# Segment-recurrent attention beside a gated MLP: output projection by column blocks, casts ahead of the transposes, and PSUM assigned by hand

## The chip, the cores and the metric

The kernel runs on one core of a Trainium2 chip. The metric is device time in microseconds: the median of three runs is 979.2 us (976.85 to 980.56). The engines are TensorE (PE; its weight loads are listed as PEld), VectorE (DVE), ScalarE (ACT), GpSimd (POOL) and SyncE (SP), which issues most DMAs.

## The reference

```python
# x (1,2048,512), mem0 (1,8,512); Wq, Wk, Wv (512,32,128); Wo (32,128,512); segments of 32 tokens
for s in range(64):
    h = concat([mem, x[:, 32*s:32*s+32]])                # 40 rows: 8 of memory, 32 of x
    q, k, v = (einsum('btd,dhe->bhte', h, W) for W in (Wq, Wk, Wv))
    scores = where(mask, q @ k.T * 128**-0.5, -1e9)      # memory rows see all, x rows causally
    o = softmax(scores) @ v
    o = einsum('bhte,hed->btd', o, Wo)
    mem = o[:, :8]; outs.append(o[:, 8:])                # the memory of the next segment
a = concat(outs)
b = gelu(layernorm(x) @ w1 + b1) @ w2 + b2               # 512 -> 1376 -> 512
g = sigmoid((x * gate_w).sum(-1)); return g * a + (1 - g) * b
```

All operands are bf16. The 64 segments are a chain: each needs the eight memory rows that the one before has put out.

## The kernel before

**MLP first.** 16 tiles of 128 tokens are taken two at a time. DVE makes the statistics of x (L114 to L117), ACT a Sqrt and a Tanh (`rstd`, L122), `prep` (L145) normalises and transposes, TensorE multiplies with w1 (L178) and w2 (L172), ACT applies Gelu (L179). `c_all` keeps (1-g)*b in SBUF for all tokens (L188). SP loads all weights in the order written; x lies whole in `x_all`.

**Setup.** Loop buffers are cleared by POOL (L214 and on), and the mask `MkA` is built by some 120 small POOL operations (L228 to L247), in four variants for the four segments of a tile.

**The loop** over 64 segments `s` (T is the tile of 128 tokens, si the segment in it) is emitted in an order written by hand, one fixed stream for each engine; `dve_q`, `act_q` and the generators `fill` and `left` hold work that is dropped in at chosen places (`flush`, `run_fill`).

- Of a segment's 40 rows, 32 (8 of memory, 24 of x) go through `qk_unit` and `v_unit`: the 32 columns of h are the stationary operand in each of the four column quadrants of TensorE, and each quadrant streams one 32-wide quarter of the heads' columns. The last 8 rows of the four segments of a tile (32 rows, the last keys) are computed a tile ahead by `left_qk` and `left_v`, as filler.
- `qk_tr` (L271): DVE transposes a bank of Q or K in 32x32 blocks from PSUM as f32 into `Tt`; ACT or POOL then casts `Tt` into QT or KT (L513), POOL into QL or KL for the last keys (L331).
- `mask_mm` puts the mask into the bank S; `scores` adds, for each of 32 heads, a matmul on the first 32 keys (L413) and one on the last keys of the whole tile (L417), of which the mask leaves this segment's 8.
- ACT takes the exponentials for memory queries (L530) and x queries (L531). TensorE sums them with a block of ones (L533, L534; L544, L545), DVE takes reciprocals (L537, L549), Pm (L539, DVE) and Px (L472, POOL) are the probabilities. `av` multiplies with V per head, main keys (L427) and last keys (L431): at once for the memory queries, a segment later for the x queries. The results go to `UTT` (L548, L485).
- Projection, `wo_unit` (L287): 32 matmuls of 512 columns. Quadrant g takes the heads with i % 4 = g, so the four quadrants hold four partial sums of all 512 columns. They are copied to `wsb` (L565 on DVE, L566 on ACT), and L575 adds the quadrants while transposing the eight memory rows; DVE writes them to the next segment's hT (L576). The x rows wait in `wsb` until a tile is complete; `out_units` adds the quadrants (L361, L370), DVE applies gate and c (L375), and one DMA stores 128 rows (L376).
- PSUM: one pool of seven banks, handed out in turn (`bank`), and one bank for S.

After the loop two sums tell whether a number left its range; a second, safe path (`tc.If`) would then compute all again.

## Time and profile before

| | us |
|---|---|
| median of three runs | 979.2 |
| span of the profiled execution | 978.4 |
| MLP on TensorE, from the first transposes to the last w2 matmul | 17.8 to 108.3 |
| from there to the first Q matmul of segment 0 | 108.3 to 138.2 |
| first Q matmul of segment 0 to that of segment 63 | 138.2 to 952.2 |
| from there to the end | 952.2 to 978.4 |

The page gives no other time of the profiled execution than its span; that lies 0.8 below the median. The page of the profile has busy times by engine, then the chain of work that ended last, then groups of instructions by source line. A row of a timeline has the start, the duration of the merged group, engine, line, operation, tiles (out<-in), the count, and in brackets how long the engine had stood idle before it and for whom.

| group | count | mean ns |
|---|---|---|
| L271 DVE transposes of 128x512 f32 | 256 | 715 |
| L485 ACT copies of U for x rows, 128x256 | 256 | 822 |
| L513 ACT casts to QT and KT, 128x512 | 128 | 618 |
| L549 DVE reciprocals, 128x256 | 64 | 1750 |
| L565, L566 copies of the projection, 128x256 | 66 each | 425, 373 |

### The profile page before, as it was taken

The page shows a single profiled execution, that of the slowest core. Times are in us where ns is not written, and L with a number is a line of the kernel's source. Part 1 is how long each engine was busy: PE and PEld are TensorE (multiplying, and loading weights), DVE is VectorE, ACT ScalarE, POOL GpSimd, SP SyncE. Part 2 cuts the span into 40 slices and gives each one's busy share as a digit, 9 for nine tenths or more (in the row PEclk, how much of TensorE's full clock was granted, in tenths as well). Part 3 has the DMA queues.
Part 4 walks back from the last instruction along what each step waited for, and adds up shares of the span by engine and source line. Part 5 has one row for each costly group of instructions (what it writes and reads, how often), then busy time and mean ns, then how long its engine had stood idle before and what let it go on. Part 6 is the DMA issues. An engine that isn't in the chain of part 4 may idle for free.

```text
span 978.4 us, 53663 instructions
## 1 busy us (share of the span) xinstructions
PE 871.1 (89%) x24969; PEld 518.0 (53%) x24977; DVE 514.7 (53%) x999; ACT 525.9 (54%) x1252; POOL 257.0 (26%) x599
## 2 busy tenths in 40 slices
PE   2999649998999999999999999989899999999996
PEld 1666315555555555555555555555555555555553
DVE  4721416554556555655565555555555545555553
ACT  2655324555555555555555555555555555555564
POOL 1000463222222232223222223222222222232320
PEclk9999779999999999999999999999999999999999
DMA  9960000000000000000000000000000000000000
GB/s 285 422 199 1 12 2 4 9 4 3 16 4 14 4 15 3 15 4 15 4 15 3 15 4 3 15 4 15 3 15 4 15 4 15 3 9 4 10 7 12
DMA packets 14996, 29.65 MB, mean 30 GB/s; under 512 B 1032, under 2 KB 12656, under 8 KB 13232
## 3 DMA queue, kind: packets, MB, share of 16 engines
q1 hardware_dynamic: 14592, 25.90, 7.4%
q8 instruction: 197, 3.23, 1.4%
q0 software_dynamic: 176, 0.27, 0.3%
q14 instruction: 31, 0.25, 0.1%
HBM read 24.06 MB, written 2.10 MB: 27 GB/s over the span
## 4 chain that ended last, share of the span: by engine, by line
PE 78%; ACT 11%; DVE 4%; issue 3%; POOL 2%; DMA 1%; SPq 1%; POOLq 0%; ACTq 0%; DVEq 0%
PE b L265 29%; PE b L287 16%; PE b L276 11%; ACT UTT L485 4%; PE b L427 4%; PE bp L172 4%; PE hp L178 3%; PE b L431 3%; ACT E L530 2%; DVE wsb L565 2%; ACT wsb L566 2%; PE S L417 2%; PE S L413 2%; PE b L533 1%; PE b L544 1%
## 5 line engine op out<-in xcount | busy, mean ns | idle before, releaser
L271 DVE STREAM_TRANSPOSE Tt<-b 128x512 f32<-128x512 f32 (+1 forms) x384 | 225.6, 613 | 111.3 <-PE b L265 82.7
L265 PEld LDWEIGHTS <-hT 128*32 128x32 bf16 x5120 | 144.3, 98 | 111.1 <-issue 14.4
L485 ACT CAST UTT<-b 128x256 bf16<-128x256 f32 x256 | 158.3, 822 | 10.8 <-PE b L431 10.5
L287 PE MATMUL b<-Wo_sb,UTT 128*32 128x512 bf16 x2624 | 161.5, 383 | 2.3 <-ACT UTT L485 1.6
L265 PE MATMUL b<-Wq_sb,hT 128*32 128x512 bf16 x2048 | 137.2, 388 | 18.7 <-POOL hT L396 13.5
L265 PE MATMUL b<-Wk_sb,hT 128*32 128x256 bf16 (+1 forms) x3072 | 137.4, 313 | 0.0
L276 PE MATMUL b<-Wv_sb,hT 128*32 128x512 bf16 x2048 | 134.5, 380 | 0.0
L472 POOL TENSOR_TENSOR Px<-E,R 128x256 bf16<-128x256 bf16 x64 | 43.2, 675 | 345.2 <-DVE R L549 345.2
L513 ACT CAST KT<-Tt 128x256 bf16<-128x256 f32 (+1 forms) x192 | 86.8, 476 | 57.4 <-DVE Tt L271 57.4
L549 DVE RECIPROCAL R<-b 128x256 f32<-128x256 f32 x64 | 112.0, 1750 | 4.5 <-PE b L545 4.5
L566 ACT CAST wsb<-b 128x256 bf16<-128x256 f32 x66 | 24.6, 373 | 157.7 <-DVE wsb L565 157.7
L287 PEld LDWEIGHTS <-UTT 128*32 128x32 bf16 x2624 | 73.0, 106 | 62.4 <-ACT UTT L485 3.5
L427 PEld LDWEIGHTS <-V 32*128 32x128 bf16 x4096 | 68.0, 91 | 58.1 <-DVE Pm L539 29.5
L537 DVE RECIPROCAL R<-b 128x64 f32<-128x64 f32 x64 | 35.7, 558 | 96.6 <-PE b L534 96.6
L513 POOL CAST QT<-Tt 128x512 bf16<-128x512 f32 x64 | 39.4, 616 | 172.4 <-DVE Tt L271 172.4
L431 PEld LDWEIGHTS <-VL 32*128 32x128 bf16 x4096 | 69.1, 91 | 13.4 <-issue 13.3
L548 ACT CAST UTT<-b 128x64 bf16<-128x64 f32 x128 | 28.5, 319 | 79.8 <-PE b L431 79.8
L276 PEld LDWEIGHTS <-hT 128*32 128x32 bf16 x2048 | 53.5, 96 | 25.9
L513 ACT CAST QT<-Tt 128x512 bf16<-128x512 f32 x64 | 39.6, 618 | 50.0 <-DVE Tt L271 49.4
L178 PE MATMUL hp<-yT,w_sb 128*128 128x256 bf16 (+1 forms) x352 | 53.0, 278 | 4.8 <-ACT hTm L179 3.1
L548 DVE CAST UTT<-b 128x64 bf16<-128x64 f32 x128 | 28.4, 301 | 54.0 <-PE b L431 54.0
L179 ACT ACTIVATE hTm<-hp,b_sb 128x256 bf16<-128x256 f32 (+1 forms) x88 | 40.6, 470 | 29.9 <-PE hp L178 29.8
(111 smaller groups left out, 1271.4 us busy)
## 6 DMA issues: line engine op xcount, KB each, us to landing
Wq_sb<-in_A_Wq_dram SPq DMA_DIRECT2D x4, 1024.0 KB, 13.0
Wk_sb<-in_A_Wk_dram SPq DMA_DIRECT2D x4, 1024.0 KB, 18.7
Wv_sb<-in_A_Wv_dram SPq DMA_DIRECT2D x4, 1024.0 KB, 20.2
Wo_sb<-in_A_Wo_dram SPq DMA_DIRECT2D x4, 1024.0 KB, 17.2
out_dram<-o SPq DMA_DIRECT2D x16, 128.0 KB, 1.7
xc<-in_A_x_dram SPq DMA_DIRECT2D x15, 128.0 KB, 2.3
x_all<-in_A_x_dram SPq DMA_DIRECT2D x3, 512.0 KB, 9.2
w_sb<-in_B_w_dram SPq DMA_DIRECT2D x1, 1376.0 KB
```

The lines of the kernel that those rows point to most:

```text
L178: nc.tensor.matmul(hp[:rows, :], lhsT=w1_sb[:, kc, fc * P:fc * P + rows], rhs=yT[:, kc, :], start=(kc == 0), stop=(kc == KC - 1))
L265: nc.tensor.matmul(bk[32 * j:32 * j + 32, 0:n], lhsT=G[:, kc, :], rhs=W5[t][:, kc, h0:h1, j, :], start=(kc == 0), stop=(kc == KC - 1), til ...
L271: nc.vector.transpose(out=Tt[:, 0:n], in_=bk[:, 0:n])
L276: nc.tensor.matmul(bk[32 * j:32 * j + 32, :], lhsT=G[:, kc, :], rhs=Wv5[:, kc, 4 * vb:4 * vb + 4, j, :], start=(kc == 0), stop=(kc == KC - ...
L287: nc.tensor.matmul(bk[32 * g:32 * g + 32, :], lhsT=lhs(i, j), rhs=Wo_sb[:, 4 * i + j, :], start=(j == 0 and i < 4), stop=(j == 3 and i >= ...
L427: nc.tensor.matmul(U[j][:, i, :], lhsT=V[q, i, :], rhs=Pt[q, i, c_main:c_main + n], start=(i == 0), stop=False, skip_group_check=True, til ...
L431: nc.tensor.matmul(U[j][:, i, u0:u0 + 8], lhsT=VL[T % 2][q, i, :], rhs=Pt[q, i, c_left:c_left + 8], start=False, stop=True, skip_group_che ...
L485: nc.scalar.copy(out=UTT[:, :, j, M:40, si], in_=U[:])
L513: (nc.gpsimd.tensor_copy if bi == 2 else nc.scalar.copy)(out=dst, in_=Tv)
L548: (nc.scalar.copy if j % 2 else nc.vector.tensor_copy)(out=UTT[:, :, j, 0:M, sp], in_=Um[j][:])
L549: nc.vector.reciprocal(out=R[:, 8 * NG:].rearrange("p (i q) -> p i q", q=32), in_=sr[:])
L566: nc.scalar.copy(out=wsb[:, 256:512], in_=wp[:, 256:512])
```

## The change

- **Projection.** `wo_group` gives each quadrant g the columns k*128 + 32*g + r (k = 0..3, r = 0..31) and all 32 heads: 128 matmuls of 128 columns. The result W[32g + token, 32k + r] is complete, so a DVE transpose of 128x128 f32 and one cast give the next hT; `wsb`, L575, the selectors and `out_units` go. `combine` applies gate and c to each segment's rows from PSUM, and four DMAs store them, in runs of 32 elements. c goes to DRAM (`c_dr`) and is loaded again by segment; gates per row come from `gseg`. The last rows get the same projection (`wo_left`), 4 loads of c and 16 stores a tile.
- **Q and K.** ACT casts a PSUM bank to bf16 with heads in pairs (`qk_cast`), DVE transposes the pairs as 4-byte elements straight into QT, KT, QL or KL. POOL no longer casts. Four banks of 16 heads stand where three of 16 and two of 8 stood.
- **Last keys.** KL and V's last keys are laid out so that the 8 last keys of four heads fill the 32 rows of one quadrant: one matmul stands for four, in `scores` and in `av`. `Mk` masks out the other heads. V's last keys are regrouped by 8 DMAs a tile.
- **PSUM by hand.** Banks U0 to U3 take Q and K, then U; X1 and X2 take V and the filler; Sb the scores; W the projection and the x queries' sums. Sums are made by quadrants.
- **Order.** The x queries' `av` moves ahead of the sums; filler units are 3, 2 and 3 in a segment and the rest behind them, where they were 5, 2, 1 and 1; x queries' reciprocals go to the start of the next segment; U's x rows are copied right after those of memory.
- **MLP and setup.** 1/sqrt by integer shift and three Newton steps on DVE, without ACT's Sqrt; x in tiles with six buffers; `prep` of the next block and its gates at fc == 1; the mask by DVE and during the MLP; two tables UT, cleared where UTT was. The check of range takes a running minimum of the reciprocals instead of sums out of the exponentials.

```diff
+    def qk_cast(bk):
+        Tb = ew.tile([P, 8, 32, 2], BF16, tag="Tb", bufs=3, name="Tb")
+        nc.scalar.copy(out=Tb[:].rearrange("p a e b -> p a b e"), in_=bk.rearrange("p (a b e) -> p a b e", a=8, b=2))
+    def qk_tr(Tb, dst, hf):
+        nc.vector.transpose(out=dst[:, 8 * hf:8 * hf + 8, 0:32, :].rearrange("p a r b -> p a (r b)").bitcast(FP32),
+                            in_=Tb[:].rearrange("p a e b -> p (a e b)").bitcast(FP32))
...
-    def wo_unit(bk, lhs, u):
-        for (j, i) in HORD[4 * u:4 * u + 4]:
-            g = i % 4
-            nc.tensor.matmul(bk[32 * g:32 * g + 32, :], lhsT=lhs(i, j), rhs=Wo_sb[:, 4 * i + j, :],
-                             start=(j == 0 and i < 4), stop=(j == 3 and i >= NG - 4), tile_position=(0, 32 * g))
+    def wo_group(bk, src, n):
+        j, i = HORD[n]
+        for g in range(4):
+            nc.tensor.matmul(bk[32 * g:32 * g + 32, 0:P], lhsT=src(j, i), rhs=Wo5[:, 4 * i + j, g],
+                             start=(n == 0), stop=(n == H - 1), tile_position=(0, 32 * g))
...
+            for si in range(SPT):
+                nc.sync.dma_start(VP[T % 2][:, si, vb, :], VL[si:P:SPT, 4 * vb:4 * vb + 4, :])
...
+        for j in range(4):
+            a0 = 8 * i2 + j // 2
+            nc.tensor.matmul(Sb[32 * j:32 * j + 32, 4 * i2:4 * i2 + 4, :].rearrange("p i (a b) -> p i a b", b=8)[:, :, 0:7:6, :],
+                             lhsT=KL[T % 2][:, si, j // 2, i2].rearrange("p l a b -> p (l a) b")[:, :, j % 2],
+                             rhs=QT[:, a0:a0 + 7:2, :, j % 2].rearrange("p a (x q) -> p a x q", q=8)[:, :, 0:5:4, :],
+                             start=False, stop=True, skip_group_check=True, tile_position=(0, 32 * j))
...
+    def combine(s):
+        nc.vector.scalar_tensor_tensor(out=o[:], in0=W[:, 0:P], scalar=gseg[:, si, T:T + 1], in1=cs.pop(s)[:], op0=ALU.mult, op1=ALU.add)
+        for g in range(4):
+            nc.sync.dma_start(out4[seg * s:seg * s + RIDE, :, g, :], o[32 * g + M:32 * g + 32, :].rearrange("p (k r) -> p k r", k=KC))
...
+            if s >= 1:
+                av(s - 1, Vs.pop(s - 1), Pxs.pop(s - 1), 64, 32, 0, 32, True)
+            sm = U[0][:, 320:384].rearrange("p (i q) -> p i q", q=8)
+            sums(sm, E, 8, 0, 8, True)
+            run(W1)
+            nc.vector.reciprocal(out=R[:, 0:8 * NG], in_=U[0][:, 320:384])
...
+        for n in range(24):
+            wo_group(W, u_main(s), n)
+        if s < nseg:
+            sums(W[:, P:P + 32 * NG].rearrange("p (i q) -> p i q", q=32), E, 16, 48, 32, False)
+        for n in range(24, H):
+            wo_group(W, u_main(s), n)
+        if s + 1 < nseg:
+            Tm = cw.tile([P, KC, 32], FP32, tag="Tm", name="Tm")
+            nc.vector.transpose(out=Tm[:].rearrange("p k q -> p (k q)"), in_=W[:, 0:P])
+            nc.vector.tensor_copy(out=hn[:, :, 0:M], in_=Tm[:, :, 0:M])
+        if s >= 2:
+            combine(s - 2)
+        if s + 1 < nseg:
+            mask_mm()
+        if s < nseg:
+            run(W3)
```

## The prediction

> **What bounds the kernel now.** I read the page's busy times and chain first, then the table of busy time by stage, then the waits of TensorE, then timelines of single segments.

> ```profile
> span 978.4 us, 53663 instructions
> ...
> PE 871.1 (89%) x24969; PEld 518.0 (53%) x24977; DVE 514.7 (53%) x999; ACT 525.9 (54%) x1252; POOL 257.0 (26%) x599
> ...
> PE 78%; ACT 11%; DVE 4%; issue 3%; POOL 2%; DMA 1%; SPq 1%; POOLq 0%; ACTq 0%; DVEq 0%
> ```

> TensorE is busy 89% and carries 78% of the chain, so its instruction stream sets the time, and the other engines count where TensorE waits for them. The stages, by timelines: the MLP to 108, a gap to 138, 64 segments, an end.

> ```profile
> 108.00:138.00 30.00, 8.71 (x111) 3.77 (x109) 9.97 (x17) 2.61 (x4) 22.37 (x126) 0.65 0.04 10
> ...
> 190.00:952.00 762.00, 713.24 (x22354) 421.43 (x22354) 425.05 (x792) 429.35 (x1048) 210.08 (x421) 0.99 0.03 8
> ```

> Columns are the stretch, its length, then busy time of PE, PEld, DVE, ACT, POOL. In the gap TensorE works 8.7 of 30 us while POOL works 22. In the loop ACT and DVE are each busy 56%.

> The first and the last segment start with these Q matmuls, so 63 segments take 952.22 - 138.24 = 814 us, 12.92 each; the rest is 138.2 ahead and 26.2 behind:

> ```profile
> 138.24 1.90 PE L265 MATMUL b<-Wq_sb,hT 128*32 128x512 bf16 x16 [13.49 <-POOL hT L396]
> ...
> 952.22 1.05 PE L265 MATMUL b<-Wq_sb,hT 128*32 128x512 bf16 x16
> ```

> One segment (from 500.92 to 513.55) shows how its 12.63 us are spent:

> ```profile
> 506.94 0.19 PE L534 MATMUL b<-E,BO 128*128 128x64 bf16 x1
> 507.06 1.05 PE L265 MATMUL b<-Wq_sb,GL 128*32 128x512 bf16 x16
> 507.94 0.39 PE L265 MATMUL b<-Wk_sb,GL 128*32 128x512 bf16 x4
> ...
> 508.26 0.18 PE L427 MATMUL b<-Pm,V 32*128 32x8 bf16 x4
> 508.30 0.17 PE L431 MATMUL b<-Pm,VL 32*128 32x8 bf16 x4
> ...
> 512.35 0.24 PE L575 MATMUL b<-Sel,wsb 128*128 128x8 bf16 x4
> 512.45 0.35 PE L404 MATMUL S<-MkA,ident 128*128 128x448 bf16 x1
> 512.99 0.40 PE L265 MATMUL b<-Wq_sb,GL 128*32 128x512 bf16 x4 [0.19 <-ACT UTT L485]
> 513.55 0.81 PE L265 MATMUL b<-Wq_sb,hT 128*32 128x512 bf16 x9 [0.17 <-ACT UTT L485]
> ```

> Durations include each matmul's latency, so I use differences of starts. Four 512-column matmuls in the four quadrants (a group) take 0.865/4 = 0.216 us, four of 256 columns 0.88/8 = 0.110: by the line through both, four of 128 columns take 0.057. Four tiny ones (8 to 40 columns) take 0.025 to 0.035, 0.031 on average, whatever their width. Each change between quadrant, row-tile and whole-array matmuls adds about 0.1 (506.94 to 507.06 for a 64-column matmul). After L404 TensorE has two holes, both ended by the new memory rows: L404's 448 columns are streamed by 512.64, yet Q starts at 513.55 with only 0.22 of filler between.

> **The change on TensorE, per segment.** Kept: Q and K 3.46, V 1.73, mask 0.19. Scores go from 64 to 40 matmuls, 0.50 to 0.31. Each attention-times-V goes from 64 to 40, 0.48 to 0.31, twice. Sums 0.38 to 0.20. The gather L575 (0.10) goes, and so does the output assembly (L361, L370; two groups a tile, 0.11 a segment). The output projection turns 8 groups of 512 columns (1.73) into 32 groups of 128, 32 x 0.057 = 1.82. Filler is 24 groups a tile for the last keys' Q, K and V (5.2), input transposes 0.2 and the last rows' projection 1.82: 7.2 a tile, 1.8 a segment. Sum after: 3.46 + 1.73 + 0.19 + 0.31 + 0.62 + 0.20 + 1.82 + 1.80 = 10.1. The same count before is 10.95, so waits and mode changes are 2.0 of its 12.92.

> **Waits after.** Mode changes fall to four, 0.4. Between row sums and Pm stand the reciprocal (0.56) and the product (0.29): 1.32 from sums to the first row-tile matmul (506.94 to 508.26). After the change 3 filler units (0.65) stand there instead of 5, so about 0.5 of wait. The copies of U take 0.54 from the last matmul to the second copy's start on DVE and 0.43 of filler covers it: 0.1. At the end the chain is shorter: projection, one DVE transpose of 128x128, one cast, Q. The transposes of 256 and 512 columns take 0.41 and 0.72, so 0.25 for 128; with 0.2 for latency ahead, 0.06 between, 0.15 for the cast and 0.17 behind, 0.85. Mask (0.19) and the three filler units left (0.65) fill 0.84 of it, so nothing is left. Without that filler, as in the last tile, 0.65 would show. Sum: 10.1 + 0.4 + 0.5 + 0.1 = 11.1.

> **ACT** gains work: it casts every Q and K bank and writes with a 4-byte step, which no row shows. From below, a contiguous 512-element copy, 0.56 in a row of them. From above, the U copies with an 8-byte step:

> ```profile
> 504.89 0.73 ACT L513 CAST KT<-Tt 128x256 bf16<-128x256 f32 x2 [0.59 <-DVE Tt L271]
> ...
> 512.19 2.47 ACT L485 CAST UTT<-b 128x256 bf16<-128x256 f32 x4
> ```

> Four strided copies take 2.47, one 0.82, so 0.55 apart; contiguous ones 0.33 (0.73 - 0.40). The step costs 0.22/256 = 0.86 ns an element, so 1.00 us for 512. I take 0.78, as the step lies between the two rows. ACT then has per segment U copies 2.6, V 1.0, exp 0.5 (its two accumulator reads go, 0.39), casts 4 x 0.78 = 3.1, last keys 1.05: 8.2 of 11.1. At 0.78 the fourth cast and its transpose end at 4.9 us into the segment, just as TensorE comes to the second half of the scores (scores start after Q, K and 24 V matmuls, 4.75): I add 0.1. At 1.00 the two last-key casts, which stand ahead of the four in half the segments, push it out by 1.5: 0.9 on average, +0.8 over what I take. **DVE** loses 3.5 of transposes from PSUM (225.6 in 64 segments) and gains about 2.1 of them from SBUF (five at 0.41), a minimum and the gating (0.45 and 0.25): under 7 us. **POOL** loses its 0.62 casts. **SP** issues 49 DMAs a tile in place of two: at 0.34 to 0.43 each (out L376, x_all L73) 5 us a segment; who waits is in the third rival. One more 0.1 is for the few slow segments (12.92 is the mean, 12.83 the steady tile). Taken: 11.3 a segment, 63 x 11.3 = 712.

> **Ahead of the loop.** The table loads and the Sqrt between statistics and y go; first hp matmul was at 20.45. Now two 0.69 statistics, about 11 small DVE operations at 0.15, y and transposes follow x at 2.94, with some 23 small mask operations on the same engine: hp at 9 to 12.5. But x tiles 6 up wait for buffers and may queue behind 16 MB of weights (landing till about 60 in the before trace), which could stop the MLP for up to 10. I take its end at 102 instead of 108.3 (95 to 110). The gap: POOL's 120 mask operations go to the MLP, but its memset of UTT doubles.

> ```profile
> 111.23 4.37 POOL L214 MEMSET UTT<- 128x5120 bf16 x1 [106.62 <-ACT c_all L188]
> ```

> 2.9 to that line, 2 x 4.37, small memsets 0.8, copies 1.0, and the first last-key groups as now (117.59 to 124.39, 6.8): 20.2 instead of 29.9. The loop starts at 122 (112 to 133).

> **Behind it**: 26.2 now. The last product, a recip of 1.75, U copies and two projections follow each other as before, but the last tile's 4 loads and 16 stores are issued one by one at 0.34: +5, so 31.

> **Sum**: 122 + 712 + 31 = 865 us. The profiled execution spans 978.4 and the median of the runs is 979.2, so add 1: **866**.

> **Rivals.**
> *Casts at the dear end*: 0.8 x 63 = 50, 916. For it: the only strided ACT row is slow. 10%.
> *Weight loads exposed*: each 128-column group has four loads of its own. If they don't run beside the streaming, a group takes 0.057 + 0.031 = 0.088: 40 groups (8 of them filler) x 0.031 x 63 = 78, 944. Against it: at 256 columns the loads hide. 7%. [...]
> *Slower than before: the DMA queues.* Stores in runs of 64 bytes (384 a segment and 512 a tile), V's last keys regrouped by DMA (1024 runs of 256 bytes a tile) and the loads of c make about 930 packets a segment.

> ```profile
> q1 hardware_dynamic: 14592, 25.90, 7.4%
> ...
> q0 software_dynamic: 176, 0.27, 0.3%
> ```

> 7.4% of 16 engines' span over 14592 packets is 79 ns each, 0.3% over 176 is 267 ns. At 79 the 16 engines need 4.6 a segment, hidden. At 267 they need 15.5: o and c have three buffers, so combine on DVE would wait for the stores, and all behind it: 122 + 63 x 15.5 + 31 = 1130. It decides above 13.1 x 16/930 = 225 ns. q0's packets landed in the crowded start, so I stay near 79: 9%. [...]
> *Faster*: if Pm's wait closes and casts cost 0.56, 0.6 x 63 = 38 less, 828: 9%.
> *It doesn't pay*: something evens it out, within 0.5%: 2%. Unnamed, between 945 and 974: 1%.

> **Chances.** The forecast (836 to 905) 62%, the rivals as given. The range 830 to 945 holds the forecast, both dear ends and about half of the faster case, a bit over 8 in 10. Faster by over 0.5% (about what a measurement of this kernel can tell from no change) 0.89, within it 0.02, slower 0.09.

> **What would show it.** Starts of a segment's first Q matmul 11.3 apart; projection groups 0.057 apart; ACT casts 0.56 to 1.0 apart; a wait of TensorE for Pm near 0.5 in each segment and almost none for hT; loop start near 122. A segment of 13 us, combine waiting for DMA, or TensorE waiting for Tb's transposes in most segments would make it wrong.

## The result and the profile after

The changed kernel takes 1048.0 us (1046.74 to 1049.05, 4 runs) against 978.0 for the kernel before (974.06 to 980.56): a ratio of 1.071 (95% interval 1.067 to 1.074). It is slower, where 866 was forecast. Page of the changed kernel, whose profiled execution took 1048.3:

```profile
span 1046.5 us, 60407 instructions
...
PE 825.0 (79%) x27807; PEld 530.2 (51%) x27807; DVE 475.3 (45%) x1212; ACT 587.9 (56%) x1106; POOL 173.2 (17%) x362
...
q1 hardware_dynamic: 88260, 34.85, 12.7%
q8 instruction: 219, 3.59, 1.4%
...
PE 66%; DVE 10%; issue 9%; SPq 5%; DMA 4%; ACT 3%; POOL 1%; DVEq 0%; ACTq 0%; POOLq 0%
```

TensorE is busy 79% of a longer span, 46 us less than before, so the work did shrink and waits took its place. In the chain "issue" has gone from 3% to 9%, SP's queue from 1% to 5% and DMA from 1% to 4%. The waits of TensorE in the changed kernel (in total, times, longest):

```profile
PE W L315 <- issue: 35.0, 35, 2.3
PE Sb L431 <- DVE KT L294: 32.7, 24, 4.1
PE U L455 <- DVE Pm L586: 27.7, 55, 1.1
PE X L315 <- issue: 17.0, 16, 1.9
```

L315 is the output projection, 32 groups of 128 columns for the loop (W) and as many a tile for the last rows (X). "issue" is idle time in which TensorE waited for nothing that the profile shows. In the kernel before it came to 1.7 us, in the changed kernel to 71.

I measure the stages from one segment's first exponential to the next one's, which can be found in every kernel; in segment 0 I start at ScalarE's table load of 1.28 us right ahead of it. Before: first at 144.8, 63 steps of 12.90, 20.6 behind the last. After: first at 147.1, 63 steps of 13.40, 55.4 behind the last. The loop of the forecast, put on the same marks, is 127.2, 11.3 and 25.8; the misses are 20, 63 x 2.1 = 132 and 30 us. By the segment into which the step leads (first to fourth of a tile) the 13.40 are 14.54, 12.32, 14.54 and 12.25. Steps without last-key work at the very end take 11.1.

**The holes put down to issue.** Timeline of TensorE in the changed kernel (start, length, line, operation, count, idle time ahead of it):

```profile
561.45 0.57 PE L315 MATMUL X<-Wo_sb,UT 128*32 128x128 bf16 x26 [0.43 <-issue]
561.80 1.56 PE L315 MATMUL W<-Wo_sb,UT 128*32 128x128 bf16 x96
563.14 0.33 PE L442 MATMUL W<-E,BO 128*32 128x256 bf16 x4
563.25 0.20 PE L445 MATMUL W<-E,BO 128*32 128x64 bf16 x2
565.20 0.21 PE L445 MATMUL W<-E,BO 128*32 128x64 bf16 x2 [1.73 <-issue]
565.20 0.65 PE L315 MATMUL W<-Wo_sb,UT 128*32 128x128 bf16 x32
565.67 0.37 PE L422 MATMUL Sb<-Mk,ident 128*32 128x448 bf16 x4
565.86 1.29 PE L315 MATMUL X<-Wo_sb,UT 128*32 128x128 bf16 x80
566.98 0.81 PE L285 MATMUL U<-Wq_sb,hT 128*32 128x512 bf16 x10
568.80 0.61 PE L285 MATMUL U<-Wq_sb,hT 128*32 128x512 bf16 x6 [1.00 <-issue]
```

Count matmuls from hole to hole: 26 + 96 + 4 + 2 = 128, then 2 + 32 + 4 + 80 + 10 = 128. Each has its weight load (27807 of both on the page), so these holes are 256 instructions apart, even in the middle of four equal matmuls (L445). They are 3.75 and 3.60 us apart. The loop has 63 holes of over 0.25 us; 37 of the 62 distances between them are a multiple of 128 recorded matmuls, the others one or two short of one. Most multiples of 256 instructions have no hole.

The queue q8, of the kind "instruction", brings 3.59 MB in 219 packets of 16 KB. TensorE has 55614 recorded instructions, 254 for each packet, close to the 256 from hole to hole; so I take a packet to hold 256 of them, an estimate from these counts (219 x 256 is 56064). In the packed trace the packets here start at 562.57 and 566.32 and take 1.39 and 1.15 us, and the two holes end 1.2 and 1.3 us after they are in. All 63 holes end 1.2 to 1.6 us after such a packet.

**The late c.** SP's queue in the changed kernel:

```profile
514.82 12.69 SPq L407 DMA_DIRECT2D out_dram<-oL  x16
527.62 3.98 SPq L531 DMA_DIRECT2D out_dram<-o  x4
531.70 5.73 SPq L381 DMA_DIRECT2D VP<-VL  x8
537.48 0.62 SPq L504 DMA_DIRECT2D c<-c_dr  x1
538.15 2.86 SPq L390 DMA_DIRECT2D cL<-c_dr  x4
```

SP issues one DMA after the other here (at most 0.12 us lies between two of these rows), and 28 stores and copies, 22.4 us, stand ahead of one load of c. What VectorE does meanwhile:

```profile
534.12 0.18 DVE L616 CAST hT<-Tm 128x32 bf16<-128x32 f32 x1
540.08 0.35 DVE L529 SCALAR_TENSOR_TENSOR o<-W,gseg,c 128x128 bf16<-128x128 f32 x1 [5.78 <-DMA cL<-c_dr]
540.35 1.75 DVE L509 RECIPROCAL R<-W 128x256 f32<-128x256 f32 x1
542.01 0.39 DVE L294 STREAM_TRANSPOSE QT<-Tb 128x256 f32<-128x256 f32 x1
```

The combine L529 stands idle for 5.78 us (the profile names cL, issued right behind; the operand of L529 is c). The combine starts 2.0 us after c's issue ends, so c is late because its issue is. Behind it in order stand the reciprocal and the transposes of Q and K, and TensorE's scores wait for those:

```profile
543.75 0.28 PE L431 MATMUL Sb<-QT,KT 128*32 128x40 bf16 x16 [3.73 <-DVE KT L294]
```

All of VectorE's waits for these loads, the last one behind the loop:

```profile
DVE o L529 <- DMA c<-c_dr: 27.7, 8, 5.8
DVE o L529 <- DMA cL<-c_dr: 22.3, 5, 6.5
DVE oL L403 <- DMA cL<-c_dr: 19.5, 1, 19.5
```

### The profile page after: what moved, and what is told of

Its sections match the earlier page's. It is cut to its first block, busy times and chain, and to the rows that moved or that the text cites. A ratio compares the mean times of both kernels' runs of the same rounds, so it can differ in the third digit from the quotient of the medians.

```text
span 1046.5 us, 60407 instructions
## 1 busy us (share of the span) xinstructions
PE 825.0 (79%) x27807; PEld 530.2 (51%) x27807; DVE 475.3 (45%) x1212; ACT 587.9 (56%) x1106; POOL 173.2 (17%) x362
## 3 DMA queue, kind: packets, MB, share of 16 engines
q1 hardware_dynamic: 88260, 34.85, 12.7%
q8 instruction: 219, 3.59, 1.4%
## 4 chain that ended last, share of the span: by engine, by line
PE 66%; DVE 10%; issue 9%; SPq 5%; DMA 4%; ACT 3%; POOL 1%; DVEq 0%; ACTq 0%; POOLq 0%
PE U L285 18%; PE W L315 12%; PE X L304 11%; PE X L285 4%; PE U L455 4%; PE bp L225 4%; PE hp L232 3%; DVE R L584 3%; PE X L315 3%; PE Sb L431 2%; DVE R L509 2%; ACT Tb L290 2%; DMA c<-c_dr 2%; DVE Pm L586 2%; SPq L381 2%
## 5 line engine op out<-in xcount | busy, mean ns | idle before, releaser
L290 ACT CAST Tb<-U 128x512 bf16<-128x512 f32 x256 | 183.3, 751 | 158.6 <-PE U L285 95.1
L315 PEld LDWEIGHTS <-UT 128*32 128x32 bf16 x10496 | 164.4, 108 | 90.1 <-issue 66.8
L315 PE MATMUL W<-Wo_sb,UT 128*32 128x128 bf16 x8448 | 154.7, 224 | 38.0 <-issue 35.0
L524 ACT CAST UT<-U 128x256 bf16<-128x256 f32 x256 | 162.0, 838 | 6.3 <-PE U L459 6.3
L285 PE MATMUL U<-Wq_sb,hT 128*32 128x512 bf16 x2048 | 141.9, 381 | 7.2 <-issue 5.2
L285 PE MATMUL U<-Wk_sb,hT 128*32 128x512 bf16 x2048 | 141.7, 379 | 1.4 <-issue 1.3
L304 PE MATMUL X<-Wv_sb,hT 128*32 128x512 bf16 x2048 | 139.6, 385 | 0.0
L509 DVE RECIPROCAL R<-W 128x256 f32<-128x256 f32 x64 | 111.9, 1748 | 0.0
L294 DVE STREAM_TRANSPOSE QT<-Tb 128x256 f32<-128x256 f32 x128 | 56.2, 439 | 57.2 <-ACT Tb L290 52.8
L304 PEld LDWEIGHTS <-hT 128*32 128x32 bf16 x2048 | 58.1, 97 | 35.2
L294 DVE STREAM_TRANSPOSE KT<-Tb 128x256 f32<-128x256 f32 x128 | 57.0, 445 | 31.1 <-ACT Tb L290 30.3
L290 ACT CAST Tb<-X 128x512 bf16<-128x512 f32 x64 | 50.8, 797 | 27.7 <-PE X L285 27.3
L431 PE MATMUL Sb<-QT,KT 128*32 128x40 bf16 x2048 | 35.8, 184 | 32.8 <-DVE KT L294 32.7
L225 PE MATMUL bp<-w_sb,hTm 128*128 128x512 bf16 (+1 forms) x176 | 51.3, 394 | 12.4 <-DVE bt L245 12.3
L315 PE MATMUL X<-Wo_sb,UT 128*32 128x128 bf16 x2048 | 41.7, 224 | 21.4 <-issue 17.0
```

The lines of the kernel that those rows point to most:

```text
L225: nc.tensor.matmul(bps[tt][:], lhsT=hTm[:rows, fc, tt * P:(tt + 1) * P], rhs=w2_sb[:rows, fc, :].rearrange("p (k g r) -> p g k r", k=KC, g ...
L285: nc.tensor.matmul(bk[32 * j:32 * j + 32, :], lhsT=G[:, kc, :], rhs=W5[t][:, kc, h0:h1, j, :], start=(kc == 0), stop=(kc == KC - 1), tile_ ...
L290: nc.scalar.copy(out=Tb[:].rearrange("p a e b -> p a b e"), in_=bk.rearrange("p (a b e) -> p a b e", a=8, b=2))
L294: nc.vector.transpose(out=dst[:, 8 * hf:8 * hf + 8, 0:32, :].rearrange("p a r b -> p a (r b)").bitcast(FP32), in_=Tb[:].rearrange("p a e b ...
L304: nc.tensor.matmul(bk[32 * j:32 * j + 32, :], lhsT=G[:, kc, :], rhs=Wv5[:, kc, 4 * vb:4 * vb + 4, j, :], start=(kc == 0), stop=(kc == KC - ...
L315: nc.tensor.matmul(bk[32 * g:32 * g + 32, 0:P], lhsT=src(j, i), rhs=Wo5[:, 4 * i + j, g], start=(n == 0), stop=(n == H - 1), tile_position ...
```

## The experiments

Theory I: TensorE is fed 256 instructions at a time and can't have them at the rate that 128 pairs of load and matmul in the projection ask for. Theory S: SP's bunched DMAs make c late. Rivals: the many short packets load the DMA engines; the streamed columns, the casts or VectorE's own work are dearer than forecast.

The measurements first. "Instr." is TensorE's recorded instructions per segment in the loop, "us per 256" the loop's time for 256 of them, a mean over its wide and its narrow matmuls; both are worked out from the traces, as are the steps.

| kernel | us | ratio to before (95%) | instr. | step | us per 256 | first exp. | behind last |
|---|---|---|---|---|---|---|---|
| before | 978.0 | 1 | 755 | 12.90 | 4.37 | 144.8 | 20.6 |
| changed | 1048.0 | 1.071 (1.067–1.074) | 831 | 13.40 | 4.13 | 147.1 | 55.4 |
| e1_before_split | 1162.1 | 1.187 (1.180–1.193) | 993 | 15.72 | 4.06 | 144.2 | 26.3 |
| e2_c_early | 1018.4 | 1.037 (1.032–1.043) | 831 | 13.02 | 4.01 | 148.5 | 50.1 |
| e3_few_instr | 1021.9 | 1.042 (1.039–1.045) | 655 | 12.90 | 5.04 | 148.9 | 53.2 |
| e4_both | 911.9 | 0.929 (0.927–0.931) | 655 | 11.33 | 4.43 | 149.5 | 46.6 |
| e5_fewer_dmas | 899.6 | 0.920 (0.917–0.923) | 655 | 11.32 | 4.42 | 147.5 | 35.2 |
| e6_ct_other_queue | 1029.6 | 1.053 (1.046–1.059) | 831 | 13.46 | 4.14 | 126.7 | 55.2 |
| e7_more_instr | 1037.5 | 1.058 (1.055–1.061) | 831 | 13.33 | 4.11 | 149.5 | 48.4 |
| e8_improved | 917.6 | 0.938 (0.935–0.940) | 759 | 12.15 | 4.10 | 118.0 | 27.0 |

The kernel before took 982.2 beside e1 to e4 and 979.8 beside e5 to e8.

**e1: the kernel before with 128-column matmuls.** In `wo_unit`:

```
-        for (j, i) in HORD[4 * u:4 * u + 4]:
+        for c, (j, i) in [(c, ji) for c in range(4) for ji in HORD[4 * u:4 * u + 4]]:
-            nc.tensor.matmul(bk[32 * g:32 * g + 32, :], lhsT=lhs(i, j), rhs=Wo_sb[:, 4 * i + j, :], ...
+            nc.tensor.matmul(bk[32 * g:32 * g + 32, 128 * c:128 * c + 128], lhsT=lhs(i, j), rhs=Wo_sb[:, 4 * i + j, 128 * c:128 * c + 128], ...
```

> The kernel before, with each 512-column matmul of its output projection cut into four of 128 columns: the same columns streamed, 120 more pairs of weight load and matmul a segment (240 instructions of TensorE on some 780). Theory I (TensorE's instructions come 256 at a time, at least about 3.55 us apart, and the quadrupled pairs exceed it): (780 + 240) / 256 x 3.55 = 14.1 us a segment in place of 12.9, so about +75 us, 1040 to 1065, with idle stretches put down to issue at the projection's line, 256 instructions apart. Theory S (SP's issue of DMAs alone) and a theory that TensorE's stream alone counts: four groups of 128 columns stream in 4 x 0.057 = 0.229 us, as one of 512 does, so 978 to 990.

1162 us: the direction of I, and more than twice its size. The two waits of TensorE that lead its table, and one stretch of the projection:

```profile
PE b L287 <- issue: 51.8, 53, 2.1
PE b L431 <- issue: 28.0, 20, 2.1
```

```profile
504.61 0.87 PE L287 MATMUL b<-Wo_sb,UTT 128*32 128x128 bf16 x48 [0.29 <-issue]
```

The columns themselves are as cheap as forecast: 48 matmuls in 0.87 us, of which 0.2 is the last one's latency (one record of such a matmul lasts 0.22 us in the mean on the changed kernel's page), are 12 groups of 0.056. So the stream isn't dearer; the instructions come late. The size was off because 3.55 us per 256 is about the pace of the holes alone: those one packet apart are 3.67 apart here. The loop also has 512-column matmuls, at 0.216 us a group some 6.9 us for 256 instructions (an estimate: 32 groups), and its mean is 4.06; by the changed kernel's mean of 4.13, 993 instructions would take 16.0 us, and 15.7 was measured. Nothing else of the change is in this kernel, so splitting the projections' matmuls costs 18.7% by itself here.

**e2: c early.**

```
-        c = cw.tile([P, P], BF16, tag="c", bufs=3, name="c")
+        c = cw.tile([P, P], BF16, tag="c", bufs=6, name="c")
-            if s >= 2:
-                c_load(s - 2)
+            c_load(s)
-            if si == 1 and T >= 1:
-                cl_load(T - 1)
+            if si == 1:
+                cl_load(T)
...
```

cL gets three buffers, and the last loads behind the loop go.

> The changed kernel with the load of c two segments earlier (six buffers) and that of cL one tile earlier (three buffers): as many DMAs, as many instructions. Theory S (c stands behind the bunched stores and VP loads in SP's queue, the combine waits for it on VectorE, and the transposes of the next segment behind the combine): VectorE's waits for c (27.7 us) and cL (22.3) go, and most of TensorE's 33 us for KT; the passage into the segment that follows the bunch falls from 14.5 to about 12.3 us, 16 times, and the last cL's wait of 19.5 goes at the end: 985 to 1010. Theory I alone (instruction supply): the stores were not on the path, 1040 to 1050. A theory that the packets of the 64-byte runs load the DMA engines: waits stay within 10 us of what they were, 1040 to 1050.

All of VectorE's waits for c and cL are gone, and TensorE's for KT too. The step into the third segment falls from 14.54 to 12.56 as S says, but the time falls by only some 30 us, less than S alone would have: the others stay at 14.62, 12.63 and 12.37, at 4.01 us per 256 instructions. The end is only 5 us shorter, since SP's last 44 stores still take 39 us end to end.

**e3: few instructions.** 8 of the 32 heads' groups, with six groups of 512 columns ahead of them, whose result is overwritten. The columns streamed are as many; the other 24 heads are missing from the projected sum, in e4, e5 and e7 too:

```
+        wo_wide(W, u_main(s))
-        for n in range(24):
+        for n in range(0, 24, 4):
             wo_group(W, u_main(s), n)
...
```

> The changed kernel with 8 of the 32 heads in its output projections, and in place of the other 24 groups of 128 columns six groups of 512 columns whose result is overwritten: the columns streamed stay the same, the other heads are left out of the projected sum, and TensorE has about 180 instructions fewer a segment (682 in place of 862); DMAs as in the changed kernel. Theory I: the idle time put down to issue (71 us) nearly all goes, the passage into the first segment of a tile falls from 14.5 to about 12.3; 970 to 1000. Theory S alone: 1040 to 1050.

1021.9 us lies between the two theories' ranges. The holes go (TensorE has no wait left that is put down to issue), and the steps into the first, second and fourth segments are 11.77, 11.24 and 11.91. But the step into the third has grown from 14.54 to 16.62, since SP's bunch is as long as it was and the segments ahead of it are shorter. VectorE's waits for the loads, and TensorE's behind them:

```profile
DVE o L538 <- DMA c<-c_dr: 60.5, 10, 7.6
...
DVE o L538 <- DMA cL<-c_dr: 34.1, 5, 7.2
```

```profile
PE Sb L440 <- DVE KT L294: 80.5, 28, 6.2
```

The waits for c and cL have nearly doubled from the 50 us of the changed kernel, KT's from 32.7.

**e4: both edits.** The edits of e2 and e3 in one kernel.

> The two edits together (c and cL early; 8 of 32 heads and six wide groups in place of the others). If I and S are both at work and make up the miss of the loop: near the forecast's 11.3 us a segment, so 140 ahead + 63 x 11.5 + 40 behind = 905, 880 to 935. If one of them is all of it, the same as the better of the two runs alone. If a third thing (clock, ScalarE, VectorE) holds the segment at 12.2: 140 + 63 x 12.2 + 40 = 949 or more.

912 us and a step of 11.33, as forecast for the changed kernel (11.3). Chain of e4:

```profile
PE 80%; DVE 9%; ACT 2%; issue 2%; DMA 2%; SPq 1%; POOL 1%; DVEq 0%; ACTq 0%; POOLq 0%
```

Each edit alone gave some 30 us and both 136: either limit nearly hides behind the other. The DMAs are the same 88260 packets as in the changed kernel, 12.7% of 16 engines' 1046.5 us or 24 ns each there, so packets, casts, VectorE and ScalarE are all out as the cause of the loop's loss.

**e5: fewer DMAs in place of an earlier c.** On e3, the 16 stores of oL a tile become 4, in block order, so that the columns of these output rows stand in another order than the reference's, and the 8 copies of VP become 4:

```
-                for si in range(SPT):
-                    ...
-                    nc.sync.dma_start(out4[t0:t0 + LEFT, :, g, :], o[32 * g + si:32 * g + 32:SPT, :].rearrange(...))
+                nc.sync.dma_start(out2[T * P:(T + 1) * P, P * g:P * g + P].rearrange("(s t) c -> t s c", s=SPT)[RIDE:seg], o[32 * g:32 * g + 32, :])
```

> The kernel with few instructions (8 of 32 heads and six wide groups in the projections), c loaded as late as in the changed kernel, and fewer DMAs: 4 stores of oL a tile in place of 16 (the columns of the left rows are stored in block order), 4 of VP in place of 8. Theory S (SP issues one DMA after the other, 0.7 us each, and c comes behind them): some 12 us of SP's work go out of the first segment of a tile, whose queue of 22 us then fits into a segment; VectorE's waits for c and cL (95 us) shrink to under 15, the passage into the third segment falls from 17.0 to 11.5: 915 to 940. If the number of DMAs isn't it (the place of c in the queue alone, or its own latency): 1000 to 1022.

900 us, under the range given; a step of 11.32. Of the 95 us of the combine's waits one of 6.2 is left, and the last cL's wait falls from 19.2 to 10.3, with c loaded as late as ever. Here the packets are fewer too (71364), but e4 had all of them without a loss in the loop; so it is SP's time for all those issues that made c late. The end is 11 us shorter than in e4 as well.

**e6: ct's stores from another queue.**

```
-                nc.sync.dma_start(c_dr[:, M + T * P:M + (T + 1) * P, :].rearrange("g t c -> t g c"), ct[:])
+                nc.gpsimd.dma_start(c_dr[:, M + T * P:M + (T + 1) * P, :].rearrange("g t c -> t g c"), ct[:])
```

> The changed kernel with the MLP's stores of ct issued by GpSimd in place of SP, nothing else. Theory: in the MLP, ct's buffers come free only when their stores have left SP's queue, which holds them behind all the weight loads; TensorE's one wait of 12.3 us for bt goes, and the first exponential of the loop comes 8 to 13 us earlier (147.1 before the edit): 1035 to 1043. Rival: the MLP ends when the last x tile or weight has landed, whatever ct does: no change within 3 us.

1029.6 us. The first exponential comes 20.4 us earlier, not 8 to 13: with the 12.3 us wait for bt go two waits for y ahead of it (5.7 together), and TensorE's granted clock from 60 to 100 us is 1.00 in place of 0.79. What makes up the other 2.4 us wasn't separated. Q of the first segment starts here:

```profile
121.46 1.05 PE L285 MATMUL U<-Wq_sb,hT 128*32 128x512 bf16 x16
```

122 was forecast.

**e7: instructions with hardly any columns.** On e4, ahead of the wide groups:

```
+        for n in range(22):
+            for g in range(4):
+                nc.tensor.matmul(W[32 * g:32 * g + 32, 0:8], lhsT=u_main(s)(0, n % NG), rhs=Wo5[:, n, g, 0, 0:8], ...
```

> The kernel of 912 us (c early, few instructions) with 88 more pairs of weight load and matmul of 8 columns a segment, into W ahead of the wide groups, overwritten after: 176 instructions of TensorE more, hardly any columns, so as many instructions as the changed kernel (about 860) and as many bytes. Theory I: the segment goes back to the 13.0 us of the kernel with c early alone, 1005 to 1030, with the idle stretches put down to issue again 256 instructions apart. If only streamed time counted: four small pairs take 0.039 us in the scores, so 22 x 0.039 = 0.86 us a segment, 950 to 970.

1037.5 us, 125 more than e4 and above the range given; the step is back at 13.33, and the waits put down to issue are back, the first of them at the added line (L616):

```profile
PE W L616 <- issue: 17.0, 31, 1.5
...
PE W L315 <- issue: 9.4, 12, 1.4
```

The added pairs stream in some 0.7 us of the 2.0 a segment (one row has 17 groups in 0.73 us, less some 0.2 for the last one's latency, 0.031 apart). With as many instructions as the changed kernel, 831, the step is nearly the same, 13.33 against 13.40. With e1 this leaves no room for a dearer 128-column matmul.

**e8: the whole computation, with these causes removed.** c and cL are loaded early as in e2, VP takes 4 DMAs, ct's stores go over GpSimd's queue, sums and mask are one matmul over the whole array in place of four, less of UT is cleared, and the last stores use two queues. The last rows' projection goes back to 512-column matmuls with the heads in the quadrants, and one matmul sums the quadrants:

```
+            nc.tensor.matmul(bk[32 * g:32 * g + 32, :], lhsT=src(j, i), rhs=Wo5[:, 4 * i + j], ...
+        ...
+        nc.tensor.matmul(bk[0:32, :], lhsT=SelS[:], rhs=wl[:], start=True, stop=True)
+        ...
+        nc.sync.dma_start(out2[T * P:(T + 1) * P, :].rearrange("(s t) d -> t s d", s=SPT)[RIDE:seg], o[:])
```

> The whole computation, with what the runs so far point to: c two segments and cL a tile early; the left projection with 32 matmuls of 512 columns and one summing matmul in place of 128 of 128 columns, its rows stored by one DMA a tile in place of 16; VP by 4 DMAs in place of 8; sums and mask by one full-array matmul in place of four; ct's stores from GpSimd; a smaller memset of UT; the last stores over two queues. About 785 instructions of TensorE a segment. Theories I and S together: 785 / 256 x 3.85 = 11.8 us a segment, the first exponential at 125 to 135, 22 to 30 us behind the last: 890 to 925. If the wide left projection or the summing costs more than it saves: 930 or more.

917.6 us, 6.2% under the kernel before (interval 6.0 to 6.5%) and some 12% under the changed one. Its page:

```profile
PE 830.1 (91%) x25327; PEld 498.1 (55%) x25327; DVE 489.7 (54%) x1265; ACT 599.2 (66%) x1122; POOL 177.0 (19%) x376
...
PE 78%; issue 10%; DVE 8%; POOL 1%; DMA 1%; ACT 0%; DVEq 0%; ACTq 0%; SPq 0%; POOLq 0%
```

SP's queue is out of the chain and issue still holds 10% of it. 759 instructions in 12.15 us are 256 in 4.10, as in the other kernels with holes, though TensorE's waits put down to issue sum to 18 us here and to 71 in the changed kernel. That the supply sets this step is likely; no run takes it away to show it. Several edits went in at once, and what each is worth was not measured.

## Why the prediction was wrong, step by step

**The stream of a segment was right.** Groups of 128 columns are 0.057 apart: 96 matmuls take 1.56 us less 0.2 of latency, 24 groups, above. With both limits away (e4, e5) a segment takes 11.33 and 11.32, and 11.3 was forecast; these kernels stream the same columns by fewer instructions, and not every term of the sum was measured by itself. Pm's wait was forecast at 0.5 and is 27.7 us in 55 segments; hT's chain is hidden, as said. The casts cost less than the 0.78 taken: three in a row take 1.92 us and one 0.75, so 0.585 apart.

**What failed first is "Sum: 10.1 + 0.4 + 0.5 + 0.1 = 11.1" as the bound of TensorE.** It sums columns and waits, and nowhere counts instructions. 831 of them in 11.3 us would be 256 in 3.5 us; the kernels that starve get 256 in 4.01 to 4.14, and neighbouring holes in the changed kernel are 3.7 apart in the mean. The kernel before stood at 4.37, within 6% of that, and nothing on its page shows it: its loop has two such holes, 0.95 us together. The supply of instructions alone holds the loop at 13.0 (e2).

**The second is "at 0.34 to 0.43 each ... 5 us a segment".** Those rows were single DMAs of whole tiles. Here, by the rows of the changed kernel's timeline, c takes 0.6 us of SP, cL and VP 0.72, oL 0.74, o 0.83. A tile sums to 2.4 + 2.9 + 11.8 + 5.8 + 13.2 + 0.5 = 37 us, under the 53 of a tile, but 22 of them come at once, ahead of c. The prediction averaged over a tile what arrives in one segment. In the trace SP's slices in the loop stand end to end in such a bunch, with 0.04 us between two in the median.

**The slower rival had the right place and the wrong price.** Combine on VectorE did wait for a DMA and everything behind it with it. But it waited for the load of c, not for buffers of o, and for SP's time per issue, not for the 79 to 267 ns that a packet was given: a packet took 24 ns. Two of the signs that the prediction named came: a segment of over 13 us, and combine waiting for DMAs, 50 us.

**Ahead of the loop**, "may queue behind 16 MB of weights" was thought of for x and not for ct's stores, which were put behind the weights on the same queue. TensorE in the MLP of the changed kernel:

```profile
73.19 9.10 PE L225 MATMUL bp<-w_sb,hTm 128*128 128x512 bf16 x33 [12.28 <-DVE bt L245]
```

SP issues ct's first store only at 66.4. e6 shows that this is the whole miss of 20 us; the 20.2 forecast for the gap behind the MLP was right (19.4).

**Behind the loop**, "the last tile's 4 loads and 16 stores are issued one by one at 0.34: +5" left out the tile before, whose 16 stores are still ahead of them:

```profile
1012.40 3.37 SPq L531 DMA_DIRECT2D out_dram<-o  x4
1015.88 11.87 SPq L407 DMA_DIRECT2D out_dram<-oL  x16
1027.79 2.86 SPq L390 DMA_DIRECT2D cL<-c_dr  x4
1032.53 11.50 SPq L407 DMA_DIRECT2D out_dram<-oL  x16
```

The last rows' gating waits 19.5 us for cL, and then 16 stores at 0.72 follow. With 4 stores a tile (e5) the time behind the last exponential is 35.2, with one (e8) 27.0, where 25.8 was forecast.

**Left open** is what sets the pace. A 16 KB packet itself takes 1.4% x 16 x 1046.5 / 219 = 1.07 us. In the changed kernel the next one starts 1.0 to 2.3 us after a hole has ended, takes its 1.1, and the next hole ends 1.2 to 1.6 later; holes one packet apart are 3.3 to 4.0 us apart, 3.7 in the mean (18 pairs). From these times alone it looks as if a packet were asked for only when the one before is in use; no run shows that. The loop's 4.0 to 4.1 also holds stretches of 512-column matmuls, where 128 of them stream for some 6.9 us (an estimate, 32 groups of 0.216), so it is a mean and no constant for other kernels. Other DMA traffic isn't it, since e1 with 14592 data packets (4.06) and e2 with 88260 (4.01) agree. Nothing was tried that could change it. The changed kernel's granted clock is 0.948 in the mean, e3's 0.917 and e8's 0.993; what part of the times is due to the clock wasn't separated.

## What to carry to other kernels

Count an engine's instructions per stage as well as its columns: here cutting one matmul into four left the stream as it was (4 x 0.056 us against 0.216) and still starved TensorE (e1, 1162 us against 982), and the kernel before, at 4.37 us per 256, showed hardly a sign of it (two holes, 0.95 us). Sum a DMA queue's issue time over the stretch in which the DMAs arrive, with what stands behind them (here 22.4 us ahead of one load of c), and load early what an engine will wait for with other work behind it: VectorE's 5.78 us for c held up the transposes, and TensorE 3.73 us behind those. When one cause is removed and the time hardly moves, remove the second one as well before calling either harmless: here 30 and 26 us alone were 136 together.
